# An S5 scan with a gated channel MLP: a fourth pair of PSUM banks, split first products of w2, and a new order of all tasks

## The chip, the core and the metric

The kernel runs on one core of one Trainium2 chip. The metric is the device time of one execution in microseconds (us). The kernel before took 153.88 us as the median of 3 runs (153.77 to 154.23). TensorE is called PE here, its weight loads PEld, VectorE DVE, ScalarE ACT, GpSimd POOL, and SyncE SP; SP issues nearly all DMAs.

## What is computed

```python
xn = layernorm(x)                              # x: 1 x 2048 x 448
# branch A: a diagonal complex recurrence over the 2048 rows
Lam_bar = exp(dt * Lam);  B_bar = ((Lam_bar - 1) / Lam)[:, None] * B
h[t] = Lam_bar * h[t-1] + B_bar @ xn[t]
s = 2 * real(h @ C.T) + xn * Dskip
# branch B: an MLP with its own layernorm, 448 -> 1792 -> 448
g = silu(gelu(layernorm(xn) @ w1 + b1) @ w2 + b2)
out = x + s * g
```

Inputs and output are bf16.

## The kernel before, in words

The 2048 rows are worked in four groups of 512 (`NG = 4`), each of two blocks of 256 rows; a block's even and odd rows are kept apart (`par` 0 and 1), because the recurrence is run on pairs of rows. For each group there are these steps, each a set of tasks:

- **statistics and normalized inputs.** bn_stats on DVE (L395, for the first group L425), `xn_sb` and `xn2_sb` on DVE or ACT (L493, L494, first group L447), and their transposes `xnT` and `xn2T` by DMA (L83). Of the first group, `xn2T` is made by PE transposes (L454) and copies out of PSUM (L413), block by block, so that PE has work before any DMA transpose can be had.
- **w1 and gelu** (`mm1_run`, L803 and L807). A tile pair `j` (of 7) writes two PSUM banks; 448 = 3 x 128 + 64 rows of contraction are done with half arrays (64 rows), in a first task of 6 matmuls and a second of 8, which adds to the same banks. Then ACT applies gelu to both banks (two instructions of 512 columns). The pairs of banks are `MB = ((0,1),(2,3),(4,7),(5,6))`, of which three are used in turn. In the first group, block 0 and block 1 do tile pairs 0 to 4 apart (256 columns each), and pairs 5 and 6 together (512 columns).
- **w2** (`mm2`, L828): 14 matmuls of 448 columns into bank 5 or 6, four times in a group; DVE adds b2 (L831), then silu on ACT (groups 0 and 3, L833) or tanh and a product (groups 1 and 2, L835, L836).
- **B products** (`bu`, L731): 14 matmuls into bank 4 for each of three parts and 7 for a fourth, copied to `u_sb` (L413); then the scan on DVE (`ssm`, L746 to L757), its copy to bf16 (L413, `vs<-s_w`), and two products with the cosine and sine tables (L773 to L777), which give `h_sb`.
- **the output** (`ym`, L871 to L891): 7 matmuls on `h_sb`, with 4 on `xnT` for even rows, then products and sums on DVE or POOL, and a DMA out.

Ahead of all this, once, parameters are made on small tiles (POOL and DVE, L528 to L592), the matrices B and C are loaded, scaled and transposed by DMA (`Bn` and `BT`; `Cr`, then `CQ` and `CZ` by `combine`, L660 to L663), and `M0` (L699, L714) is a product of B and `CQ`, of four tiles.

**What sets the order.** `Plan` records tasks with the names that each reads and writes; `emit` gives every engine its instructions in the order of one list of task numbers, `ORDER`, and `SECOND` names the tasks that go to the second of two engines allowed (mostly ACT or DVE, or POOL or DVE). A task waits for semaphores of those tasks that it depends on; each engine runs its own tasks strictly in the order of the list. So a task that waits holds up all that stands behind it on its engine. DMAs are issued by SP in the list's order too.

Of the kernel before, what the change touches and what calls it, by code (L numbers as in the profile page):

```python
# [7 lines left out]
ACT = mybir.ActivationFunctionType  # L8
# [9 lines left out]
class Task:  # L18

    __slots__ = ("eng", "ins", "reads", "writes", "sem", "idx", "deps", "chain", "alts")

    def __init__(self, eng, ins, reads, writes, sem):
        self.eng, self.ins, self.reads, self.writes, self.sem = eng, ins, tuple(reads), tuple(writes), sem
        self.deps = set()
        self.chain = False
        self.alts = [(eng, ins)]
# [7 lines left out]
class Plan:  # L36
# [69 lines left out]
    def emit(self):  # L106
# [13 lines left out]
        for t in order:  # L120
# [6 lines left out]
            waits = []  # L127
            for d in sorted(t.deps, key=at.get, reverse=True):
                sem, val = done[d]
                if seen.get(sem, 0) < val:  # L130
                    waits.append((sem, val))
                    for s, v in knows[d].items():
                        learn(seen, s, v)
                    learn(seen, sem, val)
# [25 lines left out]
ORDER = [int(k) for k in """  # L160
# [17 lines left out]
""".split()]  # L178
SECOND = [int(k) for k in """
46 54 55 62 64 67 70 75 77 84 108 113 131 134 159 161 163 164 166 178 185 186 188 190 191 221 223 225 227 229 231 239 249 250 259 267 269 330 361 363  # L180
364 383 399 400 435 446 467 479 481 486 490 498 500 501 503 509 527 528 608 611
""".split()]
# [16 lines left out]
def bass_recurrent_scan__ssm_conv_s5__mixer_channel_mlp__prompt_kernel(  # L199
# [18 lines left out]
    with ExitStack() as es:  # L218
# [81 lines left out]

        def pe(fn, reads=(), writes=(), dur=0.2, prio=0):
            kb.add("pe", fn, reads, writes, dur=dur, lat=0.25, prio=prio)

        with nc.Block():
# [39 lines left out]

            def ldw1(c, prio):
                a, w = CH[c][0] * 128, CH[c][1] * 128
                ld("sp", w1_sb[:, 0:3, a:a + w], dram_ap(B_w1, a, [[F, 128], [128 * F, 3], [1, w]]), [f"w1_{c}"], 384 * w * 2, prio, dur=0.55)
                ld("sp", w1_sb[64:128, 3, a:a + w], dram_ap(B_w1, 384 * F + a, [[F, 64], [1, w]]), [f"w1r_{c}"], 64 * w * 2, prio)
                low, high = w1_sb[0:64, 3, a:a + w], w1_sb[64:128, 2, a:a + w]
                kb.either(("dve", lambda e: e.tensor_copy(low, high)), ("act", lambda e: e.activation(low, high, ACT.Copy)), [f"w1_{c}"], [f"w1c_{c}"])  # L350

# [3 lines left out]
            ldx(1, 1, S1 + 2)  # L355
            ldw1(0, S1 + 1)
            ld("pool", brows[0:3, :], dram_ap(B_b1, 256, [[512, 3], [1, 512]]), ["br0"], 3072, 0, reads=["br"])
            ld("pool", brows[3:4, 0:256], dram_ap(B_b1, 0, [[256, 1], [1, 256]]), ["br1"], 512, 0, reads=["br"])
            for c in (1, 2, 3):
                ldw1(c, S1 + 3)  # L360
            for ri, bm in enumerate((A_B_re, A_B_im)):
# [334 lines left out]
            def m0_halves(bank):  # L696
# [3 lines left out]
                       for k, m in enumerate(BM)]  # L700
                pe(fns, ["Bn0", "Bn1", "Bn60", "Bn61", "ident"] + [f"De{i}" for i in range(4)] * (not 1) + [f"CQ{k}" for k in range(7)], [f"ps{bank}"])
                k = tslot[0] % 2
# [83 lines left out]
            def mm1_run(g, b, js, pairs):  # L786
# [9 lines left out]
                def phase(j, second):  # L796
# [4 lines left out]
                    def one(k, n, h):  # L801
                        rows, d = slice(64 * h, 64 * h + 64), (0, 1, 2 + h, 3 - h)[n]
                        return lambda e: e.matmul(view(bk[k]), w1_sb[rows, d, fcol(2 * j + k)], rhs[rows, d, :, :], start=not second and n == 0, stop=second and n == 3)  # L803
                    pe([one(h if not second else 1 - h, n, h) for n in range(4 if second else 3) for h in (0, 1)],
                       xk2 + [f"w1_{c}", f"w1r_{c}"] + ([f"w1c_{c}"] if second else []), [f"ps{bk[0]}", f"ps{bk[1]}"])
                    if second:
# [17 lines left out]
            def mm2(g, b, par, prio):  # L824
                gb, q = g % 2, par * 2 + b
                n = (2 * g + b) * 2 + par
                gs, fb, bk = n % 8, n % 2, 5 + n % 2
                fns = [lambda e, fi=fi: e.matmul(psum[:, bk, 0:D], gT[:, gb, fi, q * 128:(q + 1) * 128], w2_sb[:, fi, :],  # L828
                                                 start=(fi == 0), stop=(fi == NF - 1)) for fi in range(NF)]
# [28 lines left out]
            def ym(g, b, par, prio):  # L858
# [9 lines left out]
                def part(c0, c1):  # L868
# [4 lines left out]
                    if par == 0:  # L873
                        fns += [lambda e, d=d: e.matmul(psum[:, bk, c0:c1], xnT[:, gx, d, xs], M0[:, d, c0:c1], start=False, stop=(d == 3)) for d in range(4)]  # L874
                        du, rk = 2.1, [f"M0{d}" for d in range(4)] + [f"M0{d}d" for d in range(3)] * 1 + [f"CZ{k}" for k in range(7)]
                    else:
# [49 lines left out]
            if N1 < 7:  # L926
                mm1_run(0, None, range(N1, 7), [j % NP for j in range(N1, 7)])
            mm1_run(0, 1, range(N1), [(j + 7) % NP for j in range(N1)])
            ln_scale(0, 2 * PINNED + 3, (1,))
# [91 lines left out]
```

## Time and profile before

| | us |
|---|---|
| median of 3 runs | 153.88 |
| the profiled execution | 153.85 |
| its span, first to last instruction | 152.1 |
| PE busy | 147.3 |
| DVE busy | 128.0 |
| ACT busy | 98.7 |
| POOL busy | 41.2 |

The span is what the profile's clock covers; some 1.75 us lie around it. The page gives PE's granted clock as full (9 of 9 tenths) in all slices. A row of a timeline reads: start, length, engine, source line, operation, out<-in, count, and in brackets the idle time ahead of it and what ended it. Rows of equal instructions that follow each other are merged, and the length of a merged row runs from the first start to the last end. In the chain of waits, each row is a start, a length and the engine that the chain went through.

### The profile page before, as it was taken

Reading aid. Unit: us, or ns where it says so; the run is one execution under the profiler, and the core shown is the slowest. Engines: PE = TensorE matmul, PEld = TensorE weight load, DVE = VectorE, ACT = ScalarE, POOL = GpSimd, SP = SyncE. Lnnn points to the kernel's source line nnn. Section 1 sums busy time; section 2 is a strip of 40 time slices with the busy share of each in tenths; the row PEclk is TensorE's granted clock in tenths of the full one; section 3 lists DMA queues with packets and bytes.
Section 4 is the critical chain, followed back from the end, with each engine's and each line's share of the span. In section 5 each row is a group of like instructions: output and inputs, shape, how many; then the busy total and the mean of one; then the engine's idle time right before and its main releaser. Section 6 shows DMA issues by size and latency. Waiting matters only on the chain.

```text
span 152.1 us, 2990 instructions
## 1 busy us (share of the span) xinstructions
PE 147.3 (97%) x1136; PEld 87.1 (57%) x1136; DVE 128.0 (84%) x270; ACT 98.7 (65%) x182; POOL 41.2 (27%) x100
## 2 busy tenths in 40 slices
PE   7999999999999999999999999999999999999992
PEld 7786745444566577544444556764444666555561
DVE  3964999995999979999999996379968727999984
ACT  3887996978789549997898610463579834067400
POOL 5376817153020820010456006200071030000200
PEclk9999999999999999999999999999999999999999
DMA  4999999989896300700004032610340001100022
GB/s 118 264 286 390 253 201 189 192 150 138 149 276 173 67 0 0 138 0 4 0 0 63 4 60 47 151 60 4 60 105 17 4 0 60 60 0 0 4 100 81
DMA packets 31236, 14.73 MB, mean 97 GB/s; under 512 B 24752, under 2 KB 30774, under 8 KB 31222
## 3 DMA queue, kind: packets, MB, share of 16 engines
q1 hardware_dynamic: 30912, 14.26, 41.7%
q0 software_dynamic: 160, 0.23, 0.8%
q8 instruction: 9, 0.15, 0.4%
q10 hardware_dynamic: 150, 0.05, 0.1%
q14 instruction: 5, 0.04, 0.1%
HBM read 6.89 MB, written 1.84 MB: 57 GB/s over the span
## 4 chain that ended last, share of the span: by engine, by line
PE 84%; DMA 7%; SPq 5%; DVE 1%; issue 1%; DVEq 0%
PE psum L828 28%; PE psum L803 21%; PE psum L731 14%; PE psum L871 12%; DMA w_sb<-in_B_w_dram 7%; SPq L84 5%; PE psum L874 4%; PE psum L714 3%; PE psum L877 1%; DVE t L885 1%; DVE tmp L891 1%; PE psum L699 1%; DVEq L136 0%
## 5 line engine op out<-in xcount | busy, mean ns | idle before, releaser
L803 PE MATMUL psum<-xn2T,w_sb 64*128 64x512 bf16 (+1 forms) x462 | 44.8, 345 | 0.2
L828 PE MATMUL psum<-w_sb,gT 128*128 128x448 bf16 x224 | 44.4, 353 | 0.3 <-DMA w_sb<-in_B_w_dram 0.3
L807 ACT ACTIVATE gT<-psum,b1f 128x512 bf16<-128x512 f32 (+1 forms) x66 | 36.0, 623 | 10.7 <-PE psum L803 10.4
L803 PEld LDWEIGHTS psum<-xn2T,w_sb 64*128 64x128 bf16 x462 | 24.3, 109 | 19.6 <-ACT gT L807 2.0
L828 PEld LDWEIGHTS psum<-w_sb,gT 128*128 128x128 bf16 x224 | 21.6, 98 | 20.6 <-issue 0.9
L413 ACT ACTIVATE u_sb<-psum 128x512 bf16<-128x512 f32 (+2 forms) x22 | 10.5, 478 | 23.0 <-PE psum L731 22.7
L731 PE MATMUL psum<-xnT,BT 128*128 128x256 bf16 x196 | 24.0, 273 | 0.0
L731 PEld LDWEIGHTS psum<-xnT,BT 128*128 128x128 bf16 x196 | 18.9, 98 | 5.4 <-issue 1.1
L891 POOL TENSOR_TENSOR tmp<-t,x_all 128x448 bf16<-128x448 bf16 x5 | 5.1, 1030 | 33.1 <-DVE t L888 30.7
L755 DVE TENSOR_TENSOR_SCAN s_w<-dk,vs 128x774 f32<-128x774 f32 x8 | 14.0, 1760 | 0.1
L494 ACT ACTIVATE xn_sb<-x_all,lnw 128x448 bf16<-128x448 bf16 (+2 forms) x21 | 13.1, 661 | 1.2 <-DVE xn_sb L493 1.1
L413 ACT ACTIVATE vs<-s_w 64x256 bf16<-64x256 f32 (+2 forms) x16 | 10.9, 681 | 2.6 <-DVE s_w L755 1.5
L871 PE MATMUL psum<-CZ,h_sb 128*128 128x448 bf16 x56 | 11.9, 352 | 0.0
L871 PE MATMUL psum<-CQ,h_sb 128*128 128x448 bf16 (+2 forms) x54 | 10.5, 332 | 0.0
L831 DVE TENSOR_TENSOR o<-psum,b2bc 128x448 f32<-128x448 f32 x16 | 9.7, 614 | 0.3 <-ACT WT L642 0.2
L395 DVE BATCH_NORM_STATS2 lnst<-x_all 128x6 f32<-128x448 bf16 x12 | 7.0, 615 | 2.2 <-DMA x_all<-in_A_x_dram 2.2
L871 PEld LDWEIGHTS psum<-CZ,h_sb 128*128 128x128 bf16 x56 | 5.4, 98 | 4.7 <-DVE lnmv L401 0.4
L871 PEld LDWEIGHTS psum<-CQ,h_sb 128*128 128x128 bf16 x54 | 5.1, 98 | 4.0 <-DVE t L885 0.4
L874 PE MATMUL psum<-M,xnT 128*128 128x448 bf16 x32 | 7.4, 352 | 0.0
L493 DVE TENSOR_SCALAR xn_sb<-x_all,lnw 128x448 bf16<-128x448 bf16 (+2 forms) x19 | 7.2, 413 | 0.0
L883 DVE TENSOR_TENSOR Cr<-psum,xd 128x448 f32<-128x448 f32 x7 | 4.3, 620 | 3.5 <-PE psum L877 3.4
L474 POOL TENSOR_TENSOR lnw<-lnw,mhalf 128x8 f32<-128x8 f32 x3 | 7.0, 2334 | 0.3
(160 smaller groups left out, 188.6 us busy)
## 6 DMA issues: line engine op xcount, KB each, us to landing
out_dram<-tmp SPq DMA_DIRECT2D x7, 224.0 KB, 1.9
x_all<-in_A_x_dram SPq DMA_DIRECT2D x3, 448.0 KB, 4.1
w_sb<-in_B_w_dram SPq DMA_DIRECT2D x3, 448.0 KB, 8.3
w_sb<-in_B_w_dram SPq DMA_DIRECT2D x3, 384.0 KB, 4.7
vs<-in_A_C_re_dram SPq DMA_DIRECT2D x1, 392.0 KB, 12.1
Bn<-in_A_B_im_dram SPq DMA_DIRECT2D x1, 336.0 KB, 10.5
Bn<-in_A_B_re_dram SPq DMA_DIRECT2D x1, 336.0 KB, 10.2
vs<-in_A_C_im_dram SPq DMA_DIRECT2D x1, 336.0 KB, 10.7
```

The lines of the kernel that those rows point to most:

```text
L84: return e.dma_start(out_ap, in_ap)
L413: kb.either(("act", [lambda e, o=o, i=i: e.activation(o, i, ACT.Copy) for o, i in pairs]), ("dve", [lambda e, o=o, i=i: e.tensor_copy(o, i ...
L493: on = [("dve", [lambda e, o=o, i=i: e.tensor_scalar(o, i, rs, nb, op0=ALU.mult, op1=ALU.add) for o, i in parts], 0.4, 0.12), ("act", [lam ...
L494: ("act", [lambda e, o=o, i=i: e.activation(o, i, ACT.Identity, bias=nb, scale=rs) for o, i in parts], 0.75, 0.2)]
L731: fns = [lambda e, r=r, m=m, d=d: e.matmul(psum[:, 4, r * NK:(r + 1) * NK], BT[:, m, d, :], xnT[:, gx, d, :], start=(d == 0), stop=(d == 6 ...
L755: dve(lambda e, so=so, vi=vi: e.tensor_tensor_scan(so, dk[:].rearrange("p i c -> p (i c)"), vi, 0.0, ALU.mult, ALU.add), ["v", "vl", "dk", ...
L803: return lambda e: e.matmul(view(bk[k]), w1_sb[rows, d, fcol(2 * j + k)], rhs[rows, d, :, :], start=not second and n == 0, stop=second and ...
L807: act([lambda e, k=k: e.activation(gT[:, gb, 2 * j + k, :].rearrange("p (r c) -> p r c", r=2)[:, :, cols], view(bk[k]), ACT.Gelu_apprx_tan ...
L828: fns = [lambda e, fi=fi: e.matmul(psum[:, bk, 0:D], gT[:, gb, fi, q * 128:(q + 1) * 128], w2_sb[:, fi, :], start=(fi == 0), stop=(fi == N ...
L831: dve(lambda e: e.tensor_tensor(o2[:, fb, :], psum[:, bk, 0:D], b2bc[:], ALU.add), [f"ps{bk}", "b2bc"], [f"oo{fb}"], 0.62, prio - 76)
L871: fns = [lambda e, k=k: e.matmul(psum[:, bk, c0:c1], h_sb[:, hb, k, k0:k0 + 128], cm[:, k, c0:c1], start=(k == 0), stop=False) for k in ra ...
L874: fns += [lambda e, d=d: e.matmul(psum[:, bk, c0:c1], xnT[:, gx, d, xs], M0[:, d, c0:c1], start=False, stop=(d == 3)) for d in range(4)]
```

## The change

Five things are changed.

1. **Banks.** Block 1's tile pairs 0 to 4 of the first group use the pairs of banks (1, 3, 2, 0, 1) in place of (1, 2, 0, 1, 2): one of them goes to banks 5 and 6, those of the block's transposes and of the w2 products.
2. **First w2 products.** The first of the sixteen w2 products is three tasks, of 6, 4 and 4 matmuls, each of which waits only for its own parts of w2 and its own gelus.
3. **PE after PE.** A task of PE no longer waits for an earlier PE task that it depends on, except where one of them is a half-array product (`split`): w1's, and M0's fourth tile.
4. `ldw1` can load several parts of w1 with one DMA; with `LW` as given, it does as before.
5. **Order.** `ORDER` and `SECOND` are new for the whole kernel. The list has 634 tasks in place of 632; what is computed is the same.

```diff
+        self.chain = self.split = False
...
             for d in sorted(t.deps, key=at.get, reverse=True):
+                if t.eng == d.eng == "pe" and not (t.split or d.split):
+                    continue
...
-1 14 20 0 48 10 17 19 21 15 2 95 27 18 96 92 28 93 22 16 25 49 5 97 13 109 94 91 110 98 105 104 26 106 100 23 99 50 51 56 6 52 66 107 3 111 101 112 57
...
+0 18 48 16 17 1 2 20 91 10 95 49 19 14 92 5 96 93 21 22 28 26 15 23 94 27 31 34 25 98 30 12 100 99 101 104 97 6 33 47 41 40 102 105 109 106 50 132 110
...
-            def ldw1(c, prio):
+            def ldw1(cs, prio):
...
+            LW = ((0,), (1,), (2,), (3,))
...
-                       xk2 + [...], [f"ps{bk[0]}", f"ps{bk[1]}"])
+                       xk2 + [...], [f"ps{bk[0]}", f"ps{bk[1]}"], split=True)
...
-                fns = [lambda e, fi=fi: e.matmul(psum[:, bk, 0:D], gT[...], w2_sb[:, fi, :],
-                                                 start=(fi == 0), stop=(fi == NF - 1)) for fi in range(NF)]
-                pe(fns, [f"gT{gb}_{fi}_{b}" for fi in range(NF)] + [f"w2_{c}" for c in range(4)], [f"ps{bk}"], 2.66, prio)
+                cuts = (0, 6, 10, NF) if n == 0 else (0, NF)
+                for a, z in zip(cuts, cuts[1:]):
+                    fns = [lambda e, fi=fi: e.matmul(psum[:, bk, 0:D], gT[...], w2_sb[:, fi, :],
+                                                     start=(fi == 0), stop=(fi == NF - 1)) for fi in range(a, z)]
+                    pe(fns, [f"gT{gb}_{fi}_{b}" for fi in range(a, z)] + [f"w2_{c}" for c in sorted(set(chunk[a:z]))], [f"ps{bk}"], 2.66, prio)
...
-            mm1_run(0, 0, range(N1), [j % NP for j in range(N1)])
+            PR = ((0, 1, 2, 0, 1), (2, 0), (1, 3, 2, 0, 1))
+            mm1_run(0, 0, range(5), PR[0])
             first_apply(1)
...
-            mm1_run(0, 1, range(N1), [(j + 7) % NP for j in range(N1)])
+            mm1_run(0, None, range(5, 7), PR[1])
+            mm1_run(0, 1, range(5), PR[2])
```

What the new lists move, as the two programs' orders show:

- **Head.** DVE does all four bn_stats and bn_aggr of the first group ahead of the four normalizations (before, block 0 was normalized ahead of block 1's last statistics). PE does the transposes of both blocks ahead of the first w1 product; before, block 1's eight transposes stood behind 42 matmuls of w1. The small part of w1 is loaded first, and w2's second and first parts ahead of its third and fourth.
- **First group.** The 6 matmuls of w2's first task stand ahead of the last 28 of w1, the other 8 behind them, 4 ahead of and 4 behind the second w2 product.
- **Loads.** The 56 KB load of B's last 64 rows (imaginary part, `Bn61`) is issued behind the fourth BT transpose, where before it stood ahead of C's loads. The load of the third group's x stands ahead of BT0, before behind BT4.
- **M0.** PE's tasks from the first group's third B product on, before: B, M0, small B, w2, then the second group's first B product. After: B, w2, small B, M0, w2, then the second group's first B product.
- **From there to the third group's w1.** Before: M0, B, M0, B, w2, small B, half M0, w2. After: M0, B, M0, B, half M0, w2, small B. ACT has two normalizing tasks fewer in that stretch and two copies out of PSUM more.
- **Third group's w1.** The first task of banks 4 and 7 is followed at once by the second one of the same banks; before, tasks of other banks stood between.
- **Late.** The third group's fourth w2 product stands ahead of the last group's w1 in place of behind it.

More of the change, by code (lines that the diff above doesn't have):

```diff
@@ L18 @@
 class Task:
-    __slots__ = ("eng", "ins", "reads", "writes", "sem", "idx", "deps", "chain", "alts")
+    __slots__ = ("eng", "ins", "reads", "writes", "sem", "idx", "deps", "chain", "alts", "split")
     def __init__(self, eng, ins, reads, writes, sem):
@@ L26, in __init__ @@
         self.deps = set()
-        self.chain = False
+        self.chain = self.split = False
         self.alts = [(eng, ins)]
@@ L160 @@
 ORDER = [int(k) for k in """
[17 rows of a table removed]
[17 rows of a table added]
 """.split()]
 SECOND = [int(k) for k in """
-46 54 55 62 64 67 70 75 77 84 108 113 131 134 159 161 163 164 166 178 185 186 188 190 191 221 223 225 227 229 231 239 249 250 259 267 269 330 361 363
-364 383 399 400 435 446 467 479 481 486 490 498 500 501 503 509 527 528 608 611
+53 55 63 64 66 68 70 72 76 78 79 81 86 88 90 111 131 134 159 161 165 185 186 187 190 221 223 225 229 239 243 249 259 264 363 365 366 398 403 437 448
+470 480 484 496 500 502 503 508 526 530 531 577 590 598 610 613
 """.split()]
@@ L299, in act, with pe @@
             kb.add("act", fn, reads, writes, dur=dur, lat=0.2, prio=prio, table=table)
-        def pe(fn, reads=(), writes=(), dur=0.2, prio=0):
-            kb.add("pe", fn, reads, writes, dur=dur, lat=0.25, prio=prio)
+        def pe(fn, reads=(), writes=(), dur=0.2, prio=0, split=False):
+            kb.add("pe", fn, reads, writes, dur=dur, lat=0.25, prio=prio).split = split
         with nc.Block():
@@ L343, in bass_recurrent_scan__ssm_conv_s5__mixer_channel_mlp__prompt_kernel @@
             chunk = [c for c, (_, n) in enumerate(CH) for _ in range(n)]
-            def ldw1(c, prio):
[L346 to L350, printed above, removed]
+            def ldw1(cs, prio):
+                a, w = CH[cs[0]][0] * 128, sum(CH[c][1] for c in cs) * 128
+                ld("sp", w1_sb[:, 0:3, a:a + w], dram_ap(B_w1, a, [[F, 128], [128 * F, 3], [1, w]]), [f"w1_{c}" for c in cs], 384 * w * 2, prio, dur=0.55)
+                ld("sp", w1_sb[64:128, 3, a:a + w], dram_ap(B_w1, 384 * F + a, [[F, 64], [1, w]]), [f"w1r_{c}" for c in cs], 64 * w * 2, prio)
+                for c in cs:
+                    a, w = CH[c][0] * 128, CH[c][1] * 128
+                    low, high = w1_sb[0:64, 3, a:a + w], w1_sb[64:128, 2, a:a + w]
+                    kb.either(("dve", lambda e, low=low, high=high: e.tensor_copy(low, high)), ("act", lambda e, low=low, high=high: e.activation(low, high, ACT.Copy)), [f"w1_{c}"], [f"w1c_{c}"])
+            LW = ((0,), (1,), (2,), (3,))
             S1 = 10 * PINNED
@@ L355, in bass_recurrent_scan__ssm_conv_s5__mixer_channel_mlp__prompt_kernel @@
             ldx(1, 1, S1 + 2)
-            ldw1(0, S1 + 1)
+            ldw1(LW[0], S1 + 1)
             ld("pool", brows[0:3, :], dram_ap(B_b1, 256, [[512, 3], [1, 512]]), ["br0"], 3072, 0, reads=["br"])
             ld("pool", brows[3:4, 0:256], dram_ap(B_b1, 0, [[256, 1], [1, 256]]), ["br1"], 512, 0, reads=["br"])
-            for c in (1, 2, 3):
-                ldw1(c, S1 + 3)
+            for cs in LW[1:]:
+                ldw1(cs, S1 + 3)
             for ri, bm in enumerate((A_B_re, A_B_im)):
@@ L700, in m0_halves @@
                        for k, m in enumerate(BM)]
-                pe(fns, ["Bn0", "Bn1", "Bn60", "Bn61", "ident"] + [f"De{i}" for i in range(4)] * (not 1) + [f"CQ{k}" for k in range(7)], [f"ps{bank}"])
+                pe(fns, ["Bn0", "Bn1", "Bn60", "Bn61", "ident"] + [f"CQ{k}" for k in range(7)], [f"ps{bank}"], split=True)
                 k = tslot[0] % 2
@@ L804, in phase @@
                     pe([one(h if not second else 1 - h, n, h) for n in range(4 if second else 3) for h in (0, 1)],
-                       xk2 + [f"w1_{c}", f"w1r_{c}"] + ([f"w1c_{c}"] if second else []), [f"ps{bk[0]}", f"ps{bk[1]}"])
+                       xk2 + [f"w1_{c}", f"w1r_{c}"] + ([f"w1c_{c}"] if second else []), [f"ps{bk[0]}", f"ps{bk[1]}"], split=True)
                     if second:
@@ L827, in mm2 @@
                 gs, fb, bk = n % 8, n % 2, 5 + n % 2
-                fns = [lambda e, fi=fi: e.matmul(psum[:, bk, 0:D], gT[:, gb, fi, q * 128:(q + 1) * 128], w2_sb[:, fi, :],
-                                                 start=(fi == 0), stop=(fi == NF - 1)) for fi in range(NF)]
-                pe(fns, [f"gT{gb}_{fi}_{b}" for fi in range(NF)] + [f"w2_{c}" for c in range(4)], [f"ps{bk}"], 2.66, prio)
+                cuts = (0, 6, 10, NF) if n == 0 else (0, NF)
+                for a, z in zip(cuts, cuts[1:]):
+                    fns = [lambda e, fi=fi: e.matmul(psum[:, bk, 0:D], gT[:, gb, fi, q * 128:(q + 1) * 128], w2_sb[:, fi, :],
+                                                     start=(fi == 0), stop=(fi == NF - 1)) for fi in range(a, z)]
+                    pe(fns, [f"gT{gb}_{fi}_{b}" for fi in range(a, z)] + [f"w2_{c}" for c in sorted(set(chunk[a:z]))], [f"ps{bk}"], 2.66, prio)
                 dve(lambda e: e.tensor_tensor(o2[:, fb, :], psum[:, bk, 0:D], b2bc[:], ALU.add), [f"ps{bk}", "b2bc"], [f"oo{fb}"], 0.62, prio - 76)
@@ L874, in part @@
                         fns += [lambda e, d=d: e.matmul(psum[:, bk, c0:c1], xnT[:, gx, d, xs], M0[:, d, c0:c1], start=False, stop=(d == 3)) for d in range(4)]
-                        du, rk = 2.1, [f"M0{d}" for d in range(4)] + [f"M0{d}d" for d in range(3)] * 1 + [f"CZ{k}" for k in range(7)]
+                        du, rk = 2.1, [f"M0{d}" for d in range(4)] + [f"M0{d}d" for d in range(3)] + [f"CZ{k}" for k in range(7)]
                     else:
@@ L923, in bass_recurrent_scan__ssm_conv_s5__mixer_channel_mlp__prompt_kernel @@
             N1, NP = 5, 3
-            mm1_run(0, 0, range(N1), [j % NP for j in range(N1)])
+            PR = ((0, 1, 2, 0, 1), (2, 0), (1, 3, 2, 0, 1))
+            mm1_run(0, 0, range(5), PR[0])
             first_apply(1)
-            if N1 < 7:
-                mm1_run(0, None, range(N1, 7), [j % NP for j in range(N1, 7)])
-            mm1_run(0, 1, range(N1), [(j + 7) % NP for j in range(N1)])
+            mm1_run(0, None, range(5, 7), PR[1])
+            mm1_run(0, 1, range(5), PR[2])
             ln_scale(0, 2 * PINNED + 3, (1,))
```

32 rows, old and new, of the table ORDER are left out of this document.

## The prediction

> **What bounds the kernel now.** I read the page's busy times first, then the chain of waits in order of time, then PE's timeline at the start.
>
> ```profile
> PE 147.3 (97%) x1136; PEld 87.1 (57%) x1136; DVE 128.0 (84%) x270; ACT 98.7 (65%) x182; POOL 41.2 (27%) x100
> ```
>
> ```profile
> 30.32 10.04 PE psum L803 x83
> 40.36 1.64 PE psum L731 x14
> ...
> 59.24 1.53 PE psum L731 x14
> 60.77 2.65 PE psum L828 x14
> 63.41 0.76 PE psum L731 x7
> ...
> 67.81 9.87 PE psum L803 x86
> ...
> 146.98 0.77 PE psum L874 x4
> ```
>
> ```profile
> 6.78 2.48 PE L803 MATMUL psum<-xn2T,w_sb 64*128 64x256 bf16 x42
> 9.19 0.62 PE L454 MATMUL psum<-ident,xn_sb 128*128 128x128 bf16 x8
> 9.75 9.49 PE L803 MATMUL psum<-xn2T,w_sb 64*128 64x256 bf16 x126
> 19.56 10.75 PE L828 MATMUL psum<-w_sb,gT 128*128 128x448 bf16 x56 [0.33 <-DMA w_sb<-in_B_w_dram]
> ```
>
> PE is the bound: from 19.56 the chain goes through PE without a break up to 147.75. So the order can gain in three places only: before the first w1 product (6.78), in the waits of the first w1 stage (6.78 to 19.56), and in the tail behind 147.75. Everywhere else a new order can only keep PE busy or lose. The tail's instructions are the same in both programs, and I count it at nothing.
>
> **First stage.** How much of it is waiting? The first 42 matmuls take 2.41 us up to the transposes, 57 ns each at 256 columns. The stage has 140 of these and 28 of 512 columns, at about 115 ns (9.87/86): 8.0 + 3.2 = 11.2 us. From 6.78 to 19.56 are 12.78; less 0.56 for the eight transposes, 1.0 us is lost. Two views of PEld's waits say to what:
>
> ```profile
> PEld psum L803 <- ACT gT L807: 2.0, 6, 0.5
> PEld psum L803 <- PE psum L803: 0.7, 2, 0.3
> ```
>
> Gelus free the banks late, and twice a second task follows the first of the same banks directly and waits 0.33 for it to drain. The rest is the wait for w2. The change goes at all three: a fourth pair of banks, other tasks between such pairs, and w2's first 6 matmuls ahead of the last 28 of w1. The bank waits and drains can go whole; what is late next is the start, and the 4 matmuls (0.75) behind the second w2 product, which must cover DVE's sum (about 0.65 with its release, L831) that frees bank 6 for the third: short by 0.1. Two more changes between half arrays and whole ones cost about 0.1 each (14 matmuls of L731 take 1.64 between w1 tasks against 1.53 elsewhere, by the chain's rows), together 0.2.
>
> **The head** pays for part of that.
>
> ```profile
> 1.72 0.42 SPq L84
> ```
> ```profile
> x_all<-in_A_x_dram SPq DMA_DIRECT2D x1, 224.0 KB, 2.6
> ```
> ```profile
> 5.48 0.62 DVE L425 BATCH_NORM_STATS2 lnst<-x_all 128x6 f32<-128x448 bf16 x1
> 6.02 0.30 DVE L426 BATCH_NORM_AGGREGATE lnmv<-lnst 128x2 f32<-128x6 f32 x2
> 7.43 0.70 DVE L447 TENSOR_SCALAR xn_sb<-x_all,lnmv,lnw 128x448 bf16<-128x448 bf16 x2
> ```
> ```profile
> 6.96 1.28 ACT L437 ACT_TABLE_LOAD   x1
> 8.34 2.53 ACT L807 ACTIVATE gT<-psum,b1f 128x256 bf16<-128x256 f32 x6
> ```
>
> Block 1's x lands at 1.72 + 2.6 = 4.3. After, two statistics (0.62, the next instruction 0.54 behind the start) and their aggregates end at 5.7; ACT's scale for block 1 is estimated at 0.6 (to 6.3; an ACT pass over 128x448 is 0.66 in the rows below); four normalizations end at 7.0, since block 0's now stand behind block 1's statistics; the copy of a transposed tile on DVE ends at 7.3, and block 1's transposes (0.5) come before w1: the first w1 product starts at about 7.8, 1.0 later. The transposes (0.56) are then done. So the second group's w1 starts at 7.8 + 11.2 + 10.65 (56 matmuls of w2) + 0.1 + 0.2 = 29.95 against 30.32: **-0.4**. Bounds: -1.3 if the first product isn't later than 6.9; +0.3 if the waits that the change goes at are replaced whole. The nearest row for their replacement is ACT's: its table load waits for a scale by POOL (L534) that now stands behind a step waiting for DVE's copy (7.3): load at 8.25, first gelu at 9.6 in place of 8.34. With four pairs PE asks for the first freed banks at 11.0, when that gelu is 0.5 done; later ones have margins of 0.2. I take no wait.
>
> In the head a rule speaks against the change. The first 26 matmuls before take 2.96 us, 0.114 each, the next 12 only 0.84, 0.07 each, while the granted clock's row is full from the start.
>
> ```profile
> 1.11 2.96 PE L416 MATMUL psum<-ones 128*128 128x128 bf16 x26 [1.11 <-DVE ones L307]
> 4.28 0.84 PE L416 MATMUL psum<-ones 128*128 128x128 bf16 x12
> ```
> ```profile
> PEclk9999999999999999999999999999999999999999
> ```
>
> The Trainium skill, "TensorE: Matmul & The Clock Gate" (Part 1 and Part 4), says that PE falls back to half clock after an idle window of about 3.4 us and that transposes don't count as busy. By that rule 2.3 us of transposes and waits between the last filler matmuls (5.5) and w1 are too short; the window's phase could still make it long enough. By rows alone, a slow start costs 2.96 x (1 - 0.07/0.114) = 1.1 us: a rival with a small chance.
>
> **M0.** Its first tile needs all CQ. The load Bn61 now stands in SP's queue behind x's load and eleven transposes:
>
> ```profile
> 39.35 0.59 SPq L84 DMA_DIRECT2D x_all<-in_A_x_dram  x1
> ```
> ```profile
> out_dram<-tmp SPq DMA_DIRECT2D x1, 64.0 KB, 1.6
> Bn<-in_A_B_im_dram SPq DMA_DIRECT2D x1, 56.0 KB, 10.2
> ```
> ```profile
> 33.37 0.99 DVE L661 TENSOR_SCALAR tmp<-Bn,cw 64x448 f32<-64x448 bf16 x2
> 37.30 0.68 DVE L663 SCALAR_TENSOR_TENSOR CQ<-Cr,cw,tmp 128x448 bf16<-128x448 bf16 x1
> 38.02 0.45 DVE L661 TENSOR_SCALAR tmp<-Cr,cw 128x448 f32<-128x448 bf16 x1
> ```
>
> Before, the same issues ended at 39.94; with its own (0.6) it is issued by 40.5 and lands at about 42.1 (1.6 for 64 KB). DVE stands at it in order: 0.99 for the halves, five combinations (0.6 from start to start, the last one whole), three scaled copies (0.4) and small steps make 5.9; two rounds of ACT's copies (0.66, below, for each, two for the last) with their releases, and the last combination follow, 3.5: CQ is whole 9.4 later, at 51.5. PE wants it behind the first group's third B product, a w2 product and the small B product:
>
> ```profile
> 47.10 1.69 PE L731 MATMUL psum<-xnT,BT 128*128 128x256 bf16 x14
> ```
>
> That is 47.10 + 1.53 + 2.65 + 0.76 - 0.4 = 51.65. I take **+0.1**; bounds 0 and, at the 2.6 that 224 KB took (the head's row) and 0.5 of waits on the way, +1.5.
>
> **ACT before the third group's w1** costs the most.
>
> ```profile
> 55.16 0.60 ACT L413 ACTIVATE u_sb<-psum 128x512 bf16<-128x512 f32 x1 [2.38 <-PE psum L731]
> ```
>
> ```profile
> 56.63 0.66 ACT L660 ACTIVATE tmp<-Cr,cw 128x448 f32<-128x448 bf16 x1
> 57.19 3.19 ACT L494 ACTIVATE xn_sb<-x_all,lnw 128x384 bf16<-128x384 bf16 x6
> ```
>
> ```profile
> 60.84 0.47 ACT L413 ACTIVATE M<-psum 128x256 bf16<-128x256 f32 x2
> ```
>
> ```profile
> 70.12 1.27 ACT L807 ACTIVATE gT<-psum,b1f 128x512 bf16<-128x512 f32 x2 [0.69 <-PE psum L803]
> ```
>
> From the copy of the second group's first B product (55.16) ACT works to 69.43 (70.12 - 0.69) without a pause worth counting, then waits for PE. Free of PE its first gelu would end at 69.43 + 1.27 = 70.7; PE needs those banks 42 matmuls behind 67.74, at 72.4: slack 1.7. After, ACT's list in that stretch has two normalizing tasks fewer (2 x 1.06) and a copy of M0 and one of u more (0.47 + 0.60): -1.05. PE's list has one w2 product fewer (-2.65), and asks for the banks behind 34 matmuls, not 42 (-0.9). Slack: 1.7 + 1.05 - 2.65 - 0.9 = -0.8. On the other hand, a second task now follows the first of banks 4 and 7 directly, 0.23 to 0.33 as above. That drain stands ahead of the same gelu, so the two overlap: the stage loses **0.8** against an unbroken PE. Bounds: 0.25 (the drain alone) and 1.1. I take 0.8 since every duration is of the same shape in these rows.
>
> **The rest.** PE's waits without `split` aren't late in any row, and I give them nothing. The scan's chain on DVE ends as close ahead of PE as before; the later tasks I followed leave PE covered.
>
> **Sum**, against the profiled execution of 153.85 (the median is 153.88): -0.4 + 0.1 + 0.8 = +0.5, **154.4**.
>
> **Rivals.**
> - *ACT keeps up*: the 0.8 falls to the drain's 0.25 or less, if M0's stage or DVE hands ACT its inputs earlier or if gelu's release is quicker than rows allow. For it: before had 1.7 of slack. Time 153.85 - 0.4 + 0.1 + 0.25 = 153.8, no change, not slower. It decides if ACT begins the third group's gelus less than 2.9 us behind PE's first product there.
> - *Bn61 late*: it lands at 43.5; M0 waits 1.4, then +1.8 in all: 155.6. For it: its 56 KB took 10.2 us in the crowd before, by its row; against: few loads stand ahead.
> - *The fourth pair has nothing to do*: ACT, 1.3 late with its gelus, paces the first stage; -0.4 becomes +0.3: 155.0.
> - *Slow clock at the first products*: +1.1: 155.5.
>
> **How the numbers follow.** Forecast 0.42, with 0.4 to either side; ACT keeps up 0.28; Bn61 late 0.14; fourth pair idle 0.13; slow clock 0.03. A measurement of this kernel tells about 0.3% (0.46 us) from no change: slower means over 154.34. Slower: 0.6 of the forecast (0.25) and all of the last three (0.30): 0.55. Same: the remaining 0.17, and 0.18 of the second: 0.35. Faster: 0.10, where ACT keeps up and the first stage gains its upper half. The range leaves out the best and worst tenth: 153.3 to 155.5.
>
> **What would show it.** First L803-form matmul at 7.8; the second group's w1 near 29.95; no DVE or DMA wait at M0's first tile; ACT without a pause from the second group's u copy into the third group's gelus, and PE's weight loads waiting 0.5 for a gelu there. It is wrong if that wait is missing, or if the first w1 product starts before 7.3.

## The result, and the profile after

The changed kernel takes 154.99 us, the median of 22 times, against 153.79 for the kernel before beside it: a ratio of 1.0068 (95% interval 1.0048 to 1.0089), by which it is some 1.05 us slower. Its times scatter from 154.0 to 156.8, those of the kernel before from 153.2 to 154.8. Ratios here and below leave out slow executions, more than 1.5% above the fastest of their kernel, such as the one of 156.79 here and one of 258.82 (granted clock 0.565) with Dskip's scaling on DVE; medians and the spans of times include them. The profiled execution took 154.28, against 153.85 for the profiled one before. So there are two things to explain: 0.43 between the two profiles, and 0.7 more in a common execution than in this one.

First the 0.43. From the page of the changed kernel, PE's row, and from its chain of waits (start, length, what), the pieces that answer to those of before (L809 is now w1, L836 w2, L720 M0, L882 the last products):

```profile
PE 147.4 (97%) x1136; PEld 87.5 (57%) x1136; DVE 128.9 (85%) x277; ACT 95.3 (62%) x183; POOL 38.6 (25%) x92
```

```profile
7.58 0.45 PE psum L460 x8
8.02 9.38 PE psum L809 x140
17.40 1.24 PE psum L836 x6
18.64 1.65 PE psum L809 x28
20.29 4.27 PE psum L836 x22
24.59 5.48 PE psum L836 x28
...
40.06 2.75 DMA Bn<-in_A_B_im_dram
...
51.41 0.69 DVE CQ L669
52.15 1.50 PE psum L720 x7
...
67.99 2.93 PE psum L809 x26
70.97 7.23 PE psum L809 x64
78.20 1.43 PE psum L879 x7
...
147.44 0.77 PE psum L882 x4
```

PE has the same work (147.4 against 147.3) and the chain no longer stays on it: behind 30.10 it goes through DVE, SP, the load Bn61 and DVE's combinations, and comes back to PE only at M0 (52.15). The two traces side by side, as the start of PE's first matmul of each stage:

| | before | after | difference | gained or lost on the way |
|---|---|---|---|---|
| first product of w1 | 6.78 | 7.96 | +1.18 | |
| second group's w1 | 30.25 | 30.00 | -0.25 | -1.43 |
| third group's w1 | 67.74 | 67.92 | +0.18 | +0.43 |
| third group's first output | 77.61 | 78.14 | +0.53 | +0.35 |
| end of PE's last matmul | 149.08 | 149.54 | +0.46 | -0.07 |

The first stage is unbroken: 168 matmuls in 9.38 + 1.65 = 11.03. One wait of 0.18 is left, at bank 6. The row +0.43 is one wait of 0.46 ahead of M0's first tile, where weight loads (PEld) waited 0.6 for DVE's last combination:

```profile
PEld psum L720 <- DVE CQ L669: 0.6, 1, 0.6
PEld psum L809 <- PE psum L809: 0.5, 1, 0.5
PEld psum L836 <- DVE o L839: 0.5, 1, 0.5
```

The second of these lines (each: who waits for whom, us in all, times, longest) is the drain between the two tasks of banks 4 and 7 at 70.97, in the row +0.35; the third is bank 6. A weight load runs ahead of its matmul, so PE itself loses less than these numbers say (0.46 against 0.6 at M0).

### The profile page after: what moved, and what is told of

Its sections match the earlier page's. It is cut to its first block, busy times and chain, and to the rows that moved or that the text cites. A ratio compares the mean times of both kernels' runs of the same rounds, so it can differ in the third digit from the quotient of the medians.

```text
span 152.5 us, 2990 instructions
## 1 busy us (share of the span) xinstructions
PE 147.4 (97%) x1136; PEld 87.5 (57%) x1136; DVE 128.9 (85%) x277; ACT 95.3 (62%) x183; POOL 38.6 (25%) x92
## 4 chain that ended last, share of the span: by engine, by line
PE 79%; DVE 9%; DMA 6%; SPq 3%; issue 1%; ACT 1%; DVEq 0%
PE psum L836 25%; PE psum L809 22%; PE psum L879 12%; PE psum L737 11%; DMA x_all<-in_A_x_dram 5%; PE psum L882 4%; PE psum L720 3%; SPq L83 2%; DVE CQ L669 2%; DMA Bn<-in_A_B_im_dram 2%; DVE tmp L667 2%; PE psum L885 1%; DVE lnst L401 1%; DVE lnst L431 1%; PE psum L460 1%
## 5 line engine op out<-in xcount | busy, mean ns | idle before, releaser
L836 PE MATMUL psum<-w_sb,gT 128*128 128x448 bf16 x224 | 44.6, 353 | 0.0
L809 PE MATMUL psum<-xn2T,w_sb 64*128 64x512 bf16 (+1 forms) x462 | 44.3, 345 | 0.1
L813 ACT ACTIVATE gT<-psum,b1f 128x512 bf16<-128x512 f32 (+1 forms) x66 | 36.6, 631 | 9.0 <-PE psum L809 8.8
L809 PEld LDWEIGHTS psum<-xn2T,w_sb 64*128 64x128 bf16 x462 | 24.6, 109 | 18.9 <-ACT gT L813 2.1
L836 PEld LDWEIGHTS psum<-w_sb,gT 128*128 128x128 bf16 x224 | 21.5, 98 | 20.8 <-issue 0.8
L419 ACT ACTIVATE u_sb<-psum 128x512 bf16<-128x512 f32 (+2 forms) x23 | 11.1, 483 | 20.2 <-PE psum L737 20.1
L899 POOL TENSOR_TENSOR tmp<-t,x_all 128x448 bf16<-128x448 bf16 x5 | 6.5, 1297 | 46.5 <-DVE t L896 40.4
L500 ACT ACTIVATE xn_sb<-x_all,lnw 128x384 bf16<-128x384 bf16 (+2 forms) x18 | 10.6, 642 | 0.1
L419 ACT ACTIVATE vs<-s_w 64x256 bf16<-64x256 f32 (+2 forms) x14 | 8.0, 569 | 1.5 <-DVE s_w L761 1.3
L666 ACT ACTIVATE tmp<-Cr,cw 128x448 f32<-128x448 bf16 (+1 forms) x10 | 6.6, 666 | 3.3 <-DVE CQ L669 3.2
L772 POOL TENSOR_TENSOR ang<-s_w,ang 128x16 f32<-128x16 f32 x3 | 2.2, 718 | 22.9 <-DVE ang L597 19.2
L882 PE MATMUL psum<-M,xnT 128*128 128x448 bf16 x32 | 7.4, 352 | 0.0
## 6 DMA issues: line engine op xcount, KB each, us to landing
Bn<-in_A_B_im_dram SPq DMA_DIRECT2D x1, 336.0 KB, 10.1
```

The costliest lines, as they stand in the source:

```text
L419: kb.either(("act", [lambda e, o=o, i=i: e.activation(o, i, ACT.Copy) for o, i in pairs]), ("dve", [lambda e, o=o, i=i: e.tensor_copy(o, i ...
L500: ("act", [lambda e, o=o, i=i: e.activation(o, i, ACT.Identity, bias=nb, scale=rs) for o, i in parts], 0.75, 0.2)]
L813: act([lambda e, k=k: e.activation(gT[:, gb, 2 * j + k, :].rearrange("p (r c) -> p r c", r=2)[:, :, cols], view(bk[k]), ACT.Gelu_apprx_tan ...
```

## The experiments

All are the list of tasks (`ORDER`, `SECOND`) edited, but for the first. In their profiles the line numbers are 5 higher, since their list takes more lines. Ratios are to the kernel before, with 95% intervals. The runs were made on three chips, each beside the kernel before, so ratios compare across them and times don't. On one were the changed kernel again, Bn61 early, the third group's w1 apart and the early part; on the second the parts without the order, Dskip's scaling on DVE and both kernels with three moves; on the third the others.

**The changed kernel again.** No edit.

> The changed kernel once more, beside the three runs below. Ratio to the kernel before 1.007 again. Its first profile (154.28) lies 0.7 below its median of 154.99, so one stage must take another 0.7 in a common execution. Theory A: it is the wait for CQ ahead of M0's first tile (0.5 in the first profile: Bn61's load was under way 2.75), and a second profile with a longer time shows that wait longer. Theory B: it is the head, where the first product of w1 now follows directly from the landing of block 1's x; then a longer execution shows its first w1 product later than 8.0.

Measured: 154.81, ratio 1.0055 (1.0023 to 1.0087); the profiled execution took 154.95. Neither theory holds. The first product of w1 stands at 7.87, and there is no wait for CQ at all. The time is lost at a place that neither named: the third w2 product starts at 25.52 in place of 24.59. ACT's timeline of this execution, and its DMA row for Dskip:

```profile
21.17 1.16 ACT L500 ACTIVATE xn_sb<-x_all,lnw 128x384 bf16<-128x384 bf16 x2
24.07 0.58 ACT L375 ACTIVATE dbc<-dbc 128x448 bf16<-128x448 bf16 x1 [1.74 <-DMA dbc<-in_A_Dskip_dram]
24.55 0.82 ACT L813 ACTIVATE gT<-psum,b1f 128x256 bf16<-128x256 f32 x2
25.45 1.28 ACT L622 ACT_TABLE_LOAD   x1
```

```profile
dbc<-in_A_Dskip_dram POOLq DMA_DIRECT2D x1, 112.0 KB, 8.3
```

The same stretch of the first profile, where the load took 7.1 and ACT did not wait:

```profile
21.26 1.16 ACT L500 ACTIVATE xn_sb<-x_all,lnw 128x384 bf16<-128x384 bf16 x2
22.24 0.64 ACT L375 ACTIVATE dbc<-dbc 128x448 bf16<-128x448 bf16 x1
22.71 0.90 ACT L813 ACTIVATE gT<-psum,b1f 128x256 bf16<-128x256 f32 x2
23.68 1.28 ACT L622 ACT_TABLE_LOAD   x1
```

The scaling of `dbc` (task 46) is a small step without haste: its first reader comes at 26.7. But in the new list it goes to ACT, ahead of the last gelu of the first group, and ACT works in order. The gelu ends 1.33 behind the landing, PE waits, and everything behind is late. Before the change DVE did it, at 30.97 (L370), and the last gelu ended at 21.87.

**Bn61 early.**

```diff
-146 253 207 9 121
+146 253 39 207 9 121
...
-200 211 39 187
+200 211 187
```

> The changed kernel with one DMA moved: the load Bn61 is issued ahead of C's loads, as before the change. Theory A: DVE's combinations no longer wait for it, PE begins M0's first tile at 51.7 without a wait for CQ, 0.5 earlier than the 52.15 of the first profile, and the ratio to the kernel before falls from 1.007 to 1.003 or below. Theory B: the wait for CQ goes, but the time falls by no more than 0.3, since the load wasn't what differs between executions. Rival C: C's loads, now 0.6 later, keep CQ as late as it was, and nothing changes.

Measured: 154.38, ratio 1.0038 (1.0002 to 1.0073). The wait for CQ is gone (M0 starts at 51.93 directly behind the product ahead of it), and the way from the second to the third group's w1 is 37.37, against 37.92 in the first profile: the price of 0.46 is shown. The intervals overlap, so the gain in the median is not. Times still go from 153.7 to 156.0, so this load isn't the whole of the scatter. This profile shows one more load on the edge: w1's second part landed at 8.55 (8.07 in the first profile); PE's seventh product of w1 started 0.09 behind it, as it did in two other profiles where that part was late, and came some 0.36 late.

**Third group's w1 apart.** PE's tasks alone:

```diff
-410 411 412 414 418 417 415
+410 414 412 411 418 415 417
```

> The changed kernel with one exchange on PE in the third group's w1: a task of banks 2 and 3 stands again between the first and the second task of banks 4 and 7, as before the change, and the second of 2 and 3 ahead of the third use of 0 and 1. Theory: the drain of 0.22 (PE from 70.90 to 70.97 idle where it else overlaps by 0.15) goes, and the next use of banks 0 and 1 comes 1.0 later than their gelu's end, so PE's 90 matmuls take 9.9 in place of 10.2: 0.2 to 0.35 less, ratio 1.005. Rival: the gelus, which begin 2.7 behind PE there, take the drain's place and nothing is gained.

Measured: 156.20 (six times), ratio 1.0137 (1.0093 to 1.0181): the theory falls. The exchange brought a wait of its own, for the copies out of banks 4 and 7, by which the stage is 10.87 long in place of 10.22; and this execution shows two more. PE's timeline at both ends of it, and its weight loads' waits:

```profile
12.29 0.97 PE L814 MATMUL psum<-xn2T,w_sb 64*128 64x256 bf16 x14 [0.99 <-issue]
```

```profile
69.53 0.82 PE L814 MATMUL psum<-xn2T,w_sb 64*128 64x512 bf16 x6
70.95 1.92 PE L814 MATMUL psum<-xn2T,w_sb 64*128 64x512 bf16 x16 [0.59 <-DVE M L718]
```

```profile
PEld psum L814 <- DVE M L718: 1.1, 1, 1.1
PEld psum L725 <- DVE CQ L674: 1.0, 1, 1.0
```

The first row is a DMA, though it reads "issue": the load of w1's third part landed at 12.20, 0.09 ahead of it, where it landed at 10.1 to 10.8 in the other profiles of this head, and the first product that needs it starts at 11.0 to 11.4 there. All later loads came late too, Bn61 at 44.4, and M0 waited 0.88 for CQ.

**The early part alone, and the late part alone.** The new order up to the first group's last w2 product (task 280) and the old one behind it; then the other way round.

```diff
+ORDER = new[:280 inclusive] + [k for k in old if k not in new[:280 inclusive]]
...
+ORDER = old[:280 inclusive] + [k for k in new if k not in old[:280 inclusive]]
```

> The first 30 us alone: the changed kernel's order up to the last w2 product of the first group, and from there on the order of the kernel before (the banks, the three tasks of the first w2 product and the fewer waits stay). Theory A: the second group's w1 begins at 30.05 against 30.32, M0 and the third group's w1 go as before: 153.6, ratio 0.998. Theory B: the head costs as much as the late part, since its first product hangs on x's landing: ratio 1.002 or above, although the profile may show a start of 30.05.

> The other half of the change: the order and engines of the kernel before up to the last w2 product of the first group, the changed kernel's from there on (Bn61 is loaded early then, and dbc is scaled by DVE or ACT where the order before or after has it). By the profiles the late order costs 0.1 in the changes between half arrays and whole ones ahead of M0, 0.2 for the drain in the third group's w1 and 0.1 behind it, and gains 0.1: ratio 1.001 to 1.003. If the late part is worth as much as its scheduled times say, with nothing lost, the ratio is 1.000 or below.

Measured: the early part 155.12, ratio 1.0073 (1.0040 to 1.0106); the late part 155.76 (four times), ratio 1.0125 (1.0112 to 1.0138). The early part's second w1 starts at 30.23 (Dskip's wait 1.02 on ACT, 0.47 of it on PE), and then ACT, behind with its own list, lets PE wait 0.87 more for gelus at 35.2 and 36.4. The stretch from the third group's w1 to PE's end is as before: 81.35 against 81.34. The late part shows the rest by the same measure: 81.67, 0.33 longer, as in all seven other profiles with this order there (81.62 to 81.68). But its ratio isn't the late order's price. PE's end is 2.08 later than before, and 1.11 of that is lost ahead of the second group's w1 (a wait of 1.2 and a late first product, both of which the next run explains), 0.64 at the gelus of the second group.

**The parts without the order.** Banks, w2 tasks and fewer waits as after; the order of before.

```diff
-ORDER, SECOND = after's
+ORDER, SECOND = before's, with 272 followed by 273 and 274
```

> All of the change but the order: banks in turn of four pairs, the first w2 product as three tasks one behind the other, fewer waits of PE for PE, with the task order and engines of the kernel before. Theory: without the order the parts are worth nothing that can be measured: the three tasks let the first 10 matmuls of w2 begin without the last part of w2 at most (0.3 of wait for w2 at 19.56), ratio 0.998 to 1.001. Rival: the fewer waits or the fourth pair are worth something by themselves: ratio below 0.997.

Measured: 155.11, ratio 1.0062 (1.0037 to 1.0088): neither. The new turn of banks with the old order costs by itself, as PE's weight loads show:

```profile
17.46 1.46 PEld L814 LDWEIGHTS psum<-xn2T,w_sb 64*128 64x128 bf16 x28 [1.30 <-ACT gT L818]
```

Tile pair 3 of block 1 now wants banks 0 and 1, and in the old order it comes one task behind the 512-column pair that uses them, whose gelus are not done. The late part's profile has the same wait, the longest of this row:

```profile
PEld psum L814 <- ACT gT L818: 4.6, 9, 1.3
```

That is not the whole of this profile's 1.29 over the one before. From the first product of w1 to the second group's w1 it takes 24.05, against 23.47: 0.58. The other 0.70 is lost ahead of it: the first product stands at 7.48 in place of 6.78, though the head's order is the same. PE's filler matmuls on `ones` kept their slow pace longer in this execution; the same row of the kernel before, shown in the prediction, is 0.84 long:

```profile
4.31 1.46 PE L427 MATMUL psum<-ones 128*128 128x128 bf16 x12
```

The starts of single matmuls in the traces tell when the distance between them falls from 107 to 56 ns: at 6.4 here, at 4.0 in the profile of before, and between 3.8 and 6.4 in all 14. With the order of before in the head, the first product of w1 comes the later for it: 6.78, 7.00, 7.21, 7.30 and 7.48 for 4.0, 4.2, 5.9, 6.0 and 6.4. With the new head it is at 7.87 to 8.26 for 3.8 to 5.6, without such an order. So the one profile of the kernel before has an early change of pace, and the +1.18 of the first table is more than the new head costs beside any of the other four.

So a turn of banks is no part by itself: it is worth something only with the order made for it.

**Dskip's scaling on DVE.**

```diff
-277 46 278
+277 278
...
-193 249 76
+193 46 249 76
...
+SECOND: 46
```

> The changed kernel with one small task moved: the scaling of dbc (Dskip's broadcast, L375) is done by DVE just ahead of its first reader, and no longer by ACT ahead of the last gelu of the first group. In the four profiles so far that scaling waited on ACT for its load (landed 22.1 to 24.0), the last gelu ended at 23.6 to 25.4 against 21.1 before the change, and PE's third w2 product lost 0.2, 1.2, 0.2 and 0.5. Theory D: this wait is what makes the median of the changed kernel longer than its first profile; it goes, the second group's w1 begins at 30.0 in every profile, and the ratio falls from 1.006 to 1.002. Rival A: the late load Bn61 alone makes the difference; then the ratio stays at 1.006.

Measured: ratio 1.0103 (1.0071 to 1.0136), with nine of its twelve times between 155.3 and 156.4. Its profiled execution took 154.14, one of the two short ones: there the last gelu ends 0.42 behind the load of Dskip (23.23; 22.81), not 1.33, and the second group's w1 starts at 30.08. The 0.2 that the expectation puts down to Dskip in some profiles is the wait at bank 6: it is there with the scaling on DVE too. So the step is mended and the median isn't. What the common execution of this kernel loses its 1.5 by, no profile shows; the run of all three moves narrows it down.

**w1's third part one DMA earlier.**

```diff
-94 27 31 34 25 98 30 12
+94 27 31 30 34 25 98 12
```

> The changed kernel with one DMA moved: the 384 KB load of w1's third part is issued ahead of the 64 KB one of w1's last part, 0.6 earlier. Its landing was 10.1 to 10.8 in six profiles and 12.2 in the one execution that was 156.5, where its first product waited 1.1. The two kernels with this move (and others) had 24 times of which 23 lay within 153.9 and 154.9; the kernels with the load in its place scatter from 153.7 to 156.8. Theory E: this load is what makes the median of the changed kernel 0.7 longer than its shortest profile; then this one move takes the scatter away, median 154.3 to 154.5, ratio 1.003 to 1.004. Rival: the scatter comes from dbc on ACT or from Bn61 (both still in place), and times go on from 153.8 to 156, ratio 1.006.

Measured: 155.03, ratio 1.0066 (1.0042 to 1.0090): theory E falls as the one cause. The profiled execution took 155.48, and says why: the load of Dskip landed at 24.59. ACT and PE:

```profile
24.61 0.58 ACT L380 ACTIVATE dbc<-dbc 128x448 bf16<-128x448 bf16 x1 [2.27 <-DMA dbc<-in_A_Dskip_dram]
25.10 0.82 ACT L818 ACTIVATE gT<-psum,b1f 128x256 bf16<-128x256 f32 x2
```

```profile
26.06 1.11 PE L841 MATMUL psum<-w_sb,gT 128*128 128x448 bf16 x5 [1.56 <-ACT gT L818]
```

PE's gap is 1.7, the largest of all, and the second group's w1 starts at 31.45.

**All three moves together**, and with another order of the third group's w1:

```diff
+Dskip's scaling on DVE, Bn61 early, w1's third part one DMA earlier
...
-410 411 412 414 418 417 415 421 423
+410 411 414 412 418 415 417 423 421
```

> Three moves at once on the changed kernel: dbc scaled by DVE, the load Bn61 ahead of C's loads, and the third part of w1 loaded one DMA earlier (it landed at 10.1 to 12.2, and its first product stands at 11.1). If theories A and D hold, no wait on a DMA is left on PE's path behind the head: second group's w1 at 29.9, M0 at 51.6, the end as in the first profile less 0.7: 153.5, ratio 0.997 to 1.000. If the head's late start (7.9 against 6.8) is the cost, the ratio stays above 1.003.

> The three moves of the run above, and the third group's w1 in an order without the drain: a task of banks 0 and 1 between the two of banks 4 and 7, which begin third and not second, so that ACT's copies out of banks 4 and 7 (until 69.2) are done. Theory: 0.2 less than the run above. Rival: the first gelu, then 0.35 later, or the copies, take its place: same or worse, as where the exchange was tried at the second place.

Measured: 154.19, ratio 1.0031 (1.0002 to 1.0060), and 154.30, ratio 1.0019 (0.9997 to 1.0040). What no single move did, the three do: 11 of 12 times lie between 153.9 and 154.9, and all 12 between 154.0 and 154.5. The first of these kernels ran beside that with Dskip's scaling on DVE, on one chip, and differs from it by two moved loads alone, Bn61 and w1's third part: 1.0031 against 1.0103, and the intervals lie apart. So that kernel's loss comes from where one or both of these loads stand. Since neither of them alone took the scatter away, it comes from late loads at more than one of the three places; which two moves would do wasn't tried. In the chain of the three moves PE has the first stage unbroken and M0 behind the product ahead of it, but it waits for a gelu of the second group:

```profile
33.11 2.43 ACT gT L818 x4
35.59 4.73 PE psum L814 x42
...
48.75 2.65 PE psum L841 x14
52.16 1.32 PE psum L725 x7
...
67.76 2.93 PE psum L814 x24
70.74 7.29 PE psum L814 x56
```

That wait (0.36, four gelus in a row from the table load on) is the next in line where no DMA is late. The other order of the third group moved the loss to two waits of 0.17 and 0.29 (for the copy out of bank 7, and for a gelu); its smaller ratio is inside the interval.

**The old head** in front of two of the moves, Dskip's scaling and Bn61 (w1's loads and the engines of the head's steps are as before the change), and that with the old order behind the first group.

```diff
-ORDER = the three moves'
+ORDER = old[:130 inclusive] + the rest of the three moves', in their order, but
+        PE: 124 121 142 127 125 135 146    ACT: 120 117 123 128 126
```

> The head of the kernel before, up to block 1's transposes (42 matmuls of w1 ahead of them, all loads of w1 and w2 in their old order), and behind it the changed kernel with its four pairs and three w2 tasks, with Bn61 early and dbc on DVE. Theory: the first w1 product is at 6.8 and not 7.9 to 8.0, the transposes cost 0.6 later, the gelus start 1.3 earlier, and the second group's w1 begins at 29.3 to 29.6: ratio 0.997. Rival: w2's parts, which landed at 14.9 to 19.4 in this order of loads, hold the first w2 products, and the start is at 30 again: ratio 1.002.

> As the run above up to the first group's last w2 product, and from there on the order of the kernel before. If the early stage is won and the late order is what costs 0.3, this is the best of all: ratio 0.994 to 0.996. If ACT's work behind the first group, which the kernel before had done earlier, holds the second group's gelus as in the run with the early part alone (0.9 lost there), the ratio is 1.000.

Measured: 154.30, ratio 1.0035 (1.0017 to 1.0054), and 154.32, ratio 1.0031 (1.0016 to 1.0046). The theory falls. The first product of w1 is 0.75 earlier (7.21; not 6.8, as the fillers kept the slow pace until 5.9), and the second group's w1 starts at 30.12: the eight transposes come back into the stage (0.56), with 0.15 of wait and smaller pieces. So the late first product of the new head costs next to nothing: 1.0035 and 1.0031 with the old head, 1.0031 with the new one. Behind it the first loses 0.85 in a new place, as its B loads come late:

```profile
43.44 1.69 PE L742 MATMUL psum<-xnT,BT 128*128 128x256 bf16 x14 [0.70 <-DMA BT<-Bn]
```

The second loses 1.0 at the gelus of the second group, as the early part did, and 0.7 about M0. No kernel tried is faster than the one before.

## Why the prediction was right

It said 154.4, slower, with a range of 153.3 to 155.5; its base of 153.85 times the measured ratio is 154.9. Direction and size hold. By its own steps:

- **The head.** Forecast 7.8 for the first w1 product, measured 7.96 and 7.87; ACT's table load forecast 8.25 (measured 8.39), first gelu 9.6 (9.77). Right. That this start isn't lost again is shown by the old head.
- **Slow clock.** It did not come. PE's timeline of the changed kernel at the first products:

```profile
5.18 0.45 PE L422 MATMUL psum<-ones 128*128 128x128 bf16 x5
...
7.12 0.45 PE L422 MATMUL psum<-ones 128*128 128x128 bf16 x5
7.41 0.61 PE L460 MATMUL psum<-ident,xn_sb 128*128 128x128 bf16 x8
7.96 1.27 PE L809 MATMUL psum<-xn2T,w_sb 64*128 64x256 bf16 x20
```

  That is 0.064 each with the last one's end, against 2.48 / 42 = 0.059 before: full pace from the first. The Trainium skill, "TensorE: Matmul & The Clock Gate" (Part 1), wants an idle window of about 3.4 us for the fall to half clock. The forecast put 2.3 between the filler matmuls and w1; it is less, since five more fillers stand at 7.12. So no run here puts that rule to the test. What the runs show is another thing, that the slow pace at the start ends at different times; it reached the first w1 product in the order of before, not in the new one.
- **First stage, -0.4.** Measured -0.25 in the first profile, with the second group's w1 at 30.00 (forecast 29.95; its base of 30.32 is the chain's row, where PE's timeline has 30.25): 11.03 for the w1 matmuls (forecast 11.2), and for bank 6 a wait of 0.18 (forecast 0.1). One reading behind it was wrong. The 2.0 us that weight loads waited for gelus are those of the whole kernel; in the first stage (6 to 20 us) they are a tenth of that, and drains and the wait for w2 (the second row; PE's own row names the load) made most of the 1.0:

```profile
PEld psum L803 <- PE psum L803: 0.7, 2, 0.3
PEld psum L828 <- issue: 0.6, 1, 0.6
PEld psum L803 <- ACT gT L807: 0.2, 1, 0.2
```

  The larger miss shows in the second profile: the sum took ACT's gelus as paced by PE alone ("later ones have margins of 0.2"). Task 46 on ACT, with a DMA ahead of it, wasn't costed. It makes +0.66 out of -0.25 there.
- **M0, +0.1.** Mechanism right, size short: the load's issue began at 40.06 (forecast 39.94), it took 2.75 from there in place of 0.6 + 1.6, and CQ was whole at 52.09 in place of 51.5. PE lost 0.46, so the sign "no DVE or DMA wait at M0's first tile" failed. The rival with Bn61 late by 1.4 didn't come; the execution of 156.5 had 0.88.
- **ACT ahead of the third group's w1, +0.8.** Measured 0.35. ACT's work from the copy of the second group's first B product (57.86) up to these gelus took 12.73, where the sum makes it 14.27 - 1.05 = 13.2. ACT begins them 2.67 behind PE's first product (70.59; 67.92), under the 2.9 that the rival "ACT keeps up" named: that rival's condition came true here. The first gelu ends as PE asks (71.86). The weight loads' wait for gelus that the forecast named is there (0.4 at most, from 60 to 80 us), but it costs PE less than 0.1; the drain of 0.22 is most of what is left.

```profile
PEld psum L809 <- ACT gT L813: 0.7, 2, 0.4
```

- **The rest.** From the third group's first output to the end, -0.07: nothing, as forecast.

So the sum of the first profile is -0.25 + 0.46 + 0.35 - 0.07 = 0.49, and what is left over to 0.43 are pieces under 0.1. Two terms missed by 0.4 each, in opposite directions; that they cancel is luck, and so is it that a common execution still lies in the range, since no term stood for its other 0.7. Of that 0.7, the Dskip wait is shown in the second profile (154.95): there the second group's w1 is 0.91 later than in the first, the gelus of the second group take 0.29 more, and 0.55 comes back up to the third group's w1, 0.46 of it since CQ is then no longer awaited. Late landings of w1's third part and Bn61 are shown in one execution together. How often each of them comes in a common execution stays open, as does which of the two makes the loss of the kernel with Dskip's scaling on DVE.

## What to carry to other kernels

Ahead of the work that PE waits for, an in-order engine should hold nothing that waits for a load: a step of 0.6 us without haste cost up to 1.5 here (1.7 less the 0.2 at bank 6), by standing one place ahead of a gelu. When a new order is read, follow each engine's list, not only the bottleneck's, and write beside every step which DMA it waits for. An order whose waits end within some tenths of the landing of loads loses in a common execution what its best one shows: compare the scatter of the times, and take a second profile, of the kernel before too, before the terms of one profile are believed.

## What the runs showed of the hardware

The same 112 KB broadcast took 3.9 to 4.4 us to land when it was issued at 22.5 to 24.0 (three profiles), and 7.1 to 9.0 at 15.0 to 16.3 (eleven), while C, B and the parts of w2 were under way; this row is of the kernel with w1's third part earlier:

```profile
dbc<-in_A_Dskip_dram POOLq DMA_DIRECT2D x1, 112.0 KB, 9.0
```

A load of 56 KB took 2.6 to 3.2 behind transposes on the same queue at 40 to 42, and 8.6 to 10.9 in the crowd at 9.4 to 9.7. PE's fillers at the start changed from a matmul in 107 ns to one in 56 ns between 3.8 and 6.4 us, at another time in each execution, while the page's clock row reads 9 in all slices. And a second PE task that waits on the first one's matmuls in the same banks lost 0.22 in every profile with that order (eight of them: 0.07 of idle time and the usual 0.15 of overlap between two tasks), though nothing but PE was between.
